# Attention weights of heads 16 to 29 transposed by DMA instead of TensorE, in a sorted-block attention followed by a dense mixture of experts

## The chip, the cores and the metric

The kernel runs on one core of a Trainium2 chip. Such a core has TensorE (PE in the profile: matmuls, and weight loads as PEld), VectorE (DVE), ScalarE (ACT), GpSimd (POOL), SyncE (SP, which here only issues DMAs) and 16 DMA engines. The metric is the device time of one execution in microseconds (us); several runs are taken, and their median counts.

## The reference

Four batches of 8 heads (32 heads, written g below), 768 positions, 64 columns a head. The positions form 8 blocks of 96. A sorting matrix P (8x8 for each head) is made doubly stochastic by five rounds of exponential and of row and column normalisation; it mixes the blocks of k and v; then each block of q attends to the sorted block in its place. The result, 3072 rows of 512, goes through 8 experts with weights P from a second normalisation (8 rounds). Every expert works on every row.

```python
k_sorted = einsum('bhij,bhjcd->bhicd', P, k_blocks)        # v the same
attn = softmax(q_block @ k_sorted_block.T / 8)             # 96 x 96 for each block and head
x = (attn @ v_sorted_block) as [B*S, H*D]                  # 3072 x 512
logits = x @ w_gate; P = exp(logits - max)
8 times: P /= row sums; P /= column sums; P *= N/E
out = sum over e of P[:, e] * (relu(x @ w1[e]) @ w2[e])    # 512 -> 1024 -> 512
```

Inputs and output are float32; the kernel computes its matmuls in bfloat16.

## The kernel before

The order of the instructions on every engine is the order in which the Python code emits them, up to the end of the gate's normalisation. Engines wait for each other through semaphores that the framework places for every tile. Each engine takes its own instructions strictly in order, so an instruction that waits holds whatever is behind it.

**Start.** GpSimd issues the loads of the first five pairs of heads (`load_pair`, k, v and q, cast to bfloat16 on the way). VectorE and ScalarE normalise P for all 32 heads at once.

**Attention loop.** Step s runs from 0 to 33. In it stand, in this order:

1. `scores(s)`: 8 matmuls into a psB tile (L310); VectorE takes row maxima (L315) and subtracts them (L317).
2. `a_transpose(s-1)`: 8 transposes on TensorE of the 96x96 blocks of attention weights into a psF tile (L328), and a ScalarE copy to `aT_` (L330).
3. `sort_kv(s+2)`: 6 matmuls mix the blocks of k and v (L295), ScalarE casts the result into `kvT_` (L298), and SP issues a DMA transpose that puts v into `v1_` (L301), 64 rows of 1024.
4. `weights(s)`: ScalarE's exponential into `at_` (L321).
5. On even steps `q_transpose` (L253, copies L259) and GpSimd's `relayout` (L78); on odd steps `x_transpose` of a finished pair of heads (L353, copy L356).
6. `attend(s-1)`, called AV below: 8 matmuls (L335), with a column of ones in v that gives the row sums; `normalise(s-1)` on VectorE (L343, L344).

**Buffers.** PSUM has two pools: psB with 2 buffers of two banks (scores, sort, AV in turn) and psF with 4 of one bank (all transposes, all pieces). `kvT_` holds 4 heads, `v1_` 5, `at_` and `aT_` 2 each; these are cut by hand out of one tile each, by head modulo the number. Raw pairs have 5 buffers.

**Pieces.** Expert 0 is computed inside the loop. Whenever eight heads of a batch are done, its 768 rows can be used: `add` puts a gate piece (L209), 16 first-layer pieces (L187, relu on ScalarE L190) and 6 output tiles (L198, copied to SBUF at L200) on a list, and says over how many slots they are to be spread. `fill()` stands four times in each step and is a slot: it emits pieces as their hand-given costs (0.65, 1.72, 0.7) fall due.

```python
def fill():
    if slots[0] > 0:
        ahead[0] += sum(c for c, _ in pieces) / slots[0]
        slots[0] -= 1
    while pieces and ahead[0] >= pieces[0][0] / 2:
        c, run = pieces.pop(0); run(); ahead[0] -= c
```

**Behind the loop.** The gate piece and the pieces of the fourth batch run beside the eight rounds of the gate's normalisation; then come experts 1 to 7, each with six stretches of 32 first-layer matmuls into hps (L417) and 32 second-layer ones into psF (L495). The weights have two buffers (`load_expert`, L163 and L164).

Of the kernel before, what the change touches and what calls it, by code (L numbers as in the profile page):

```python
# [12 lines left out]
BF16 = mybir.dt.bfloat16  # L13
# [6 lines left out]
def mkap(t, dims, off=0):  # L20
    return bass.AP(tensor=t.tensor, offset=t.offset + off, ap=dims)
# [3 lines left out]
def kernel(  # L25
# [11 lines left out]
    nc = tc.nc  # L37
    B, H, S, D = 4, 8, 768, 64
    NB, BL = 8, 96
    CL, CH = 6, 16  # L40
    NH = B * H
# [11 lines left out]
    pp = ctx.enter_context(tc.tile_pool(name="pp", bufs=1))  # L53
# [4 lines left out]

    rawp = ctx.enter_context(tc.tile_pool(name="rawp", bufs=5))
    iop = ctx.enter_context(tc.tile_pool(name="iop", bufs=2))
    raw_t, kv_t = {}, {}

    def load_pair(n):
        kv = rawp.tile([128, 2, 2, CL, D], BF16, name="kvr")
        qr = rawp.tile([128, 2, CL, D], BF16, name="qr")
        for t, r in ((k, kv[:, 0]), (v, kv[:, 1]), (q, qr)):
            nc.gpsimd.dma_start(
                out=r.rearrange("p h c d -> p h (c d)"),  # L70
                in_=bass.AP(tensor=t.tensor, offset=t.offset + 2 * n * S * D,
                            ap=[[CL * D, 128], [S * D, 2], [1, CL * D]]))
        raw_t[n] = (kv, qr)
# [23 lines left out]
    nc.vector.memset(P9, EPS)  # L97
    perp = ctx.enter_context(tc.tile_pool(name="perp", bufs=1))

    NKT, NVB = 4, 5  # L100
    kvT_ = perp.tile([128, NKT, NB, 128], BF16)
    nc.vector.memset(kvT_[:, :, :, 96:128], 0.0)

# [11 lines left out]
    nc.vector.memset(qT_[0:64, :, :, S:], 0.0)  # L115


    at_ = perp.tile([96, 2, S + 32], BF16)
    aT_ = perp.tile([97, 2, S + 32], BF16)
    nc.vector.memset(at_[:, :, S:], 0.0)  # L120
    nc.vector.memset(aT_[0:96, :, S:], 0.0)

    mask16 = ones.tile([128, CH], F32)
    nc.vector.reduce_sum(out=mask16, in_=If32.rearrange("p (j c) -> p c j", c=CH), axis=AX.X)
# [8 lines left out]
    for it in range(5):  # L133
# [9 lines left out]
        if it == 0:  # L143
            Ibf = ones.tile([128, 128], BF16)
# [15 lines left out]
    def load_expert(e):  # L160
        w1e = wp.tile([128, 4, F], BF16, name="w1e")
        w2e = wp.tile([128, 8, Dm], BF16, name="w2e")
        nc.gpsimd.dma_start(out=w1e, in_=moe_w1[e].rearrange("(kk k) f -> k kk f", k=128))  # L163
        nc.gpsimd.dma_start(out=w2e, in_=moe_w2[e].rearrange("(fb k) f -> k fb f", k=128))  # L164
        w1t.append(w1e)
        w2t.append(w2e)
# [14 lines left out]
    def l1_piece(c, fb):  # L181
        def run():
            if fb == 0:
                hT0[c] = mps.tile([128, 8, 512], BF16, name="hTs")
            hps = psF.tile([128, 512], F32, name="psF")
            for kk in range(4):
                nc.tensor.matmul(hps[:, 0:HC], w1t[0][:, kk, fb * 128:(fb + 1) * 128],  # L187
                                 xtT[:, kk, c * HC:(c + 1) * HC],
                                 start=(kk == 0), stop=(kk == 3))
            nc.scalar.activation(out=hT0[c][:, fb, 0:HC], in_=hps[:, 0:HC], func=AF.Relu)  # L190
        return run

    def l2_piece(c, tt, copy=nc.vector.tensor_copy):
        def run():
            t = c * 3 + tt
            oacc = psF.tile([128, Dm], F32, name="psF")
            for fb in range(8):
                nc.tensor.matmul(oacc, hT0[c][:, fb, tt * 128:(tt + 1) * 128],  # L198
                                 w2t[0][:, fb, :], start=(fb == 0), stop=(fb == 7))
            copy(osbl[:, t, :], oacc)  # L200
        return run

    def gate_piece(b):
        def run():
            gps = psF.tile([128, 512], F32, name="psF")
            for tl in range(6):
                t = b * 6 + tl
                for kk in range(4):
                    nc.tensor.matmul(gps[:, tl * E:(tl + 1) * E], xtT[:, kk, t * 128:(t + 1) * 128],  # L209
                                     wg[:, kk], start=(kk == 0), stop=(kk == 3))  # L210
            nc.vector.tensor_copy(glog[:, b * 6:(b + 1) * 6, 0:E],
                                  gps[:, 0:6 * E].rearrange("p (t e) -> p t e", e=E))
        return run

    def batch_pieces(b):

        out_ = []
        for c in (2 * b, 2 * b + 1):
            out_ += [(0.65, l1_piece(c, fb)) for fb in range(8)]
            out_ += [(1.72, l2_piece(c, tt)) for tt in range(3)]  # L220
        return out_

    pieces = []
# [2 lines left out]
    def add(more, n):  # L226

        pieces.extend(more)
        slots[0] = n
# [88 lines left out]
        ssb_t[g] = ssb  # L318

    def weights(g):  # L320
        nc.scalar.activation(out=at_[:, g % 2, 0:S].rearrange("p (i c) -> p i c", c=BL),  # L321
                             in_=ssb_t.pop(g).rearrange("p a i c -> p (a i) c"),
                             func=AF.Exp, scale=scale)

    def a_transpose(g):
        ta = psF.tile([128, NB, 96], BF16, name="psF")
        for i in range(NB):
            nc.tensor.matmul(ta[:, i, :], at_[:, g % 2, i * BL:i * BL + 128], Ibf[0:96, 0:96],  # L328
                             is_transpose=True, start=True, stop=True)
        nc.scalar.copy(aT_[0:96, g % 2, 0:S], ta[0:96].rearrange("p i c -> p (i c)"))  # L330

    def attend(g):
        ops_ = psB.tile([128, 2, 4, 128], F32, name="psB")
        for i in range(NB):
            nc.tensor.matmul(ops_[:, i // 4, i % 4, 0:65], aT_[0:97, g % 2, i * BL:i * BL + 128],  # L335
                             v1_[0:97, g % NVB, i, 0:65], start=True, stop=True)
        ops_t[g] = ops_

    def normalise(g):
        n, r0 = g // 2, 64 * (g % 2)  # L340
        ops_ = ops_t.pop(g)
        den = sp.tile([96, 2, 4], F32, name="den")
        nc.vector.reciprocal(out=den, in_=ops_[0:96, :, :, 64])  # L343
        nc.vector.tensor_mul(  # L344
            og_[:, n % 2, :, r0:r0 + 64].rearrange("p (a i) d -> p a i d", a=2),
            ops_[0:96, :, :, 0:64],
            mkap(den, [den.ap[0], [4, 2], [1, 4], [0, 64]]))

    def x_transpose(n):
        b, hp = n // 4, n % 4  # L350
        tx = psF.tile([128, NB, 96], BF16, name="psF")
        for i in range(NB):
            nc.tensor.matmul(tx[:, i, :], og_[:, n % 2, i, :], Ibf[0:96, 0:96],  # L353
                             is_transpose=True, start=True, stop=True)

        nc.scalar.copy(xtT[:, hp, b * S:(b + 1) * S].rearrange("p (i h l) -> p i h l", h=CH, l=CL),  # L356
                       tx.rearrange("p i (l h) -> p i h l", h=CH))

    build_R(nc.vector, Pps, 0, 2)
    nc.vector.tensor_copy(Pb, Pps[:, 0:256].rearrange("p (i g) -> p i g", g=32))  # L360
    nc.vector.memset(aT_[96:97], 1.0)
    sort_kv(0)
    build_R(nc.gpsimd, Pb, 2, 2)
    relayout(1)
    load_pair(5)
    nc.gpsimd.dma_start(out=wg, in_=moe_w_gate.rearrange("(kk k) e -> k kk e", k=128))
    NP = NH // 2
    for s in range(NH + 2):
        if s % 2 == 0 and s + 4 < NH:
            build_R(nc.gpsimd, Pb, s + 4, 2)  # L370
        if s < NH:
            scores(s)
        if s == 0:
            sort_kv(1)
            onesc = ones.tile([128, 128], F32)
            nc.gpsimd.memset(onesc, 1.0)
            nc.gpsimd.memset(glog[:, NT, :], EPS / 128)
            nc.gpsimd.memset(glog[:, 0:NT, E:E + 1], EPS)
        fill()
        if 0 <= s - 1 < NH:  # L380
            a_transpose(s - 1)
        fill()
        if s + 2 < NH:
            sort_kv(s + 2)
        if s < NH:
            weights(s)
        if s % 2 == 0:
            if 0 < s and s // 2 + 1 < NP:
                q_transpose(s // 2 + 1)
            if s // 2 + 2 < NP:  # L390
                relayout(s // 2 + 2)
        elif s >= 3:
            x_transpose((s - 3) // 2)
        fill()
        if 0 <= s - 1 < NH:
            attend(s - 1)
            normalise(s - 1)
        if s % 2 == 1 and s // 2 + 6 < NP:
            load_pair(s // 2 + 6)
        fill()  # L400
        if s % 8 == 1 and 1 < s < NH:
            add([(0.7, gate_piece((s - 9) // 8))] + batch_pieces((s - 9) // 8), 33)
        if s in (2, 20):
            load_expert(s // 16)
    actx.close()


# [54 lines left out]
    for it in range(8):  # L462
# [8 lines left out]
            out=gl, in0=gl, scalar=float(N) / E,  # L471
# [5 lines left out]
    for e in range(1, E):  # L477
        if e + 1 < E:
            load_expert(e + 1)
        for nc4 in range(6):  # L480
            for fb in range(AHEAD if (e, nc4) == (1, 0) else 0, 8):
                l1_tile(e, nc4, fb)
            for tt in range(4):
# [8 lines left out]
                for c0 in range(0, Dm, W):  # L492
                    oacc = psF.tile([128, Dm], F32, name="psF")
                    for fb in range(8):
# [3 lines left out]
                        out=osbl[:, t, c0:c0 + W], in0=oacc[:, 0:W],  # L498
                        scalar=glog[:, t, e:e + 1], in1=osbl[:, t, c0:c0 + W],
                        op0=ALU.mult, op1=ALU.add)  # L500
                    if e == E - 1:
                        nc.sync.dma_start(out=out[t * 128:(t + 1) * 128, c0:c0 + W],
                                          in_=osbl[:, t, c0:c0 + W])
# [30 lines left out]
```

## Time and profile before

| | |
|---|---|
| median of 3 runs | 765.98 us (765.73 to 766.4) |
| the profiled execution | 764.95 us |
| its span, first to last instruction | 763.2 us |
| mean granted TensorE clock | 0.993 |
| PE busy | 734.6 us (96%) |
| VectorE, ScalarE, GpSimd busy | 272.3, 338.6, 80.5 us (36, 44, 11%) |
| first scores; last AV of the loop | 15.9; 152.25 us |
| gate piece behind the loop | 156.29 us |
| first tile of expert 1; its second layer | 173.54; 186.3 us |

Times in a profile row are from the span's start. A timeline row reads: start, duration, engine, line, operation, what is written and read, shape, number of instructions; in brackets the idle time of the engine before it and what ended that. A row of the stretches reads: length, then for each engine the busy time and the number of instructions, the granted TensorE clock, the mean busy share of the DMA engines (counted in packets' time, so it can pass 1) and GB/s.

### The profile page before, as it was taken

The page shows a single profiled execution, that of the slowest core. Times are in us where ns is not written, and L with a number is a line of the kernel's source. Part 1 is how long each engine was busy: PE and PEld are TensorE (multiplying, and loading weights), DVE is VectorE, ACT ScalarE, POOL GpSimd, SP SyncE. Part 2 cuts the span into 40 slices and gives each one's busy share as a digit, 9 for nine tenths or more (in the row PEclk, how much of TensorE's full clock was granted, in tenths as well). Part 3 has the DMA queues.
Part 4 walks back from the last instruction along what each step waited for, and adds up shares of the span by engine and source line. Part 5 has one row for each costly group of instructions (what it writes and reads, how often), then busy time and mean ns, then how long its engine had stood idle before and what let it go on. Part 6 is the DMA issues. An engine that isn't in the chain of part 4 may idle for free.

```text
span 763.2 us, 10596 instructions
## 1 busy us (share of the span) xinstructions
PE 734.6 (96%) x4452; PEld 372.9 (49%) x4452; DVE 272.3 (36%) x466; ACT 338.6 (44%) x569; POOL 80.5 (11%) x104
## 2 busy tenths in 40 slices
PE   2779999999999999999999999999999999999998
PEld 2666666655444444444444444444444444444444
DVE  6878778666512112122121221221212212112122
ACT  7888888744342332423424334233243342432422
POOL 8954431000000000000000000000000000000000
PEclk9979999999999999999999999999999999999999
DMA  9999792205100420015000600042001500002112
GB/s 153 189 178 134 103 140 31 20 1 90 22 1 0 75 37 0 1 27 84 1 2 0 111 1 1 0 69 42 0 1 23 89 1 1 0 1 97 70 71 95
DMA packets 47231, 37.40 MB, mean 49 GB/s; under 512 B 19408, under 2 KB 40144, under 8 KB 47184
## 3 DMA queue, kind: packets, MB, share of 16 engines
q0 software_dynamic: 26128, 26.23, 22.5%
q1 hardware_dynamic: 21056, 10.50, 7.0%
q8 instruction: 35, 0.57, 0.3%
q14 instruction: 12, 0.10, 0.0%
HBM read 52.45 MB, written 6.29 MB: 77 GB/s over the span
## 4 chain that ended last, share of the span: by engine, by line
PE 93%; ACT 2%; DVE 2%; DMA 1%; issue 0%; DVEq 0%; ACTq 0%
PE psF L495 38%; PE hps L417 38%; PE psF L187 5%; PE psF L198 5%; DMA v__108<-kvT__106 1%; PE psF L328 1%; PE psB L310 1%; PE psB L295 1%; PE psB L335 1%; ACT kvT__106 L298 1%; ACT aT__115 L330 0%; DVE ssb L317 0%; PE psF L353 0%; PE psF L253 0%; DVE mx L315 0%
## 5 line engine op out<-in xcount | busy, mean ns | idle before, releaser
L420 ACT ACTIVATE hTs<-hps 128x512 bf16<-128x512 f32 x336 | 200.7, 597 | 372.8 <-PE hps L417 372.8
L417 PE MATMUL hps<-xtT,w1e 128*128 128x512 bf16 x1344 | 297.4, 379 | 0.0
L495 PE MATMUL psF<-w2e,hTs 128*128 128x512 bf16 (+1 forms) x1352 | 296.9, 378 | 0.0
L497 DVE SCALAR_TENSOR_TENSOR osbl<-psF,glog,osbl 128x512 f32<-128x512 f32 (+1 forms) x169 | 126.3, 748 | 437.6 <-PE psF L495 437.4
L495 PEld LDWEIGHTS <-hTs 128*128 128x128 bf16 x1352 | 132.4, 98 | 157.7
L417 PEld LDWEIGHTS <-w1e 128*128 128x128 bf16 x1344 | 131.5, 98 | 158.5
L187 PE MATMUL psF<-xtT,w1e 128*128 128x384 bf16 x256 | 50.7, 329 | 0.0
L163 POOL DMA_DIRECT2D w1e<-in_moe_w_dram x8 | 6.2, 774 | 420.9 <-PE hps L417 370.4
L198 PE MATMUL psF<-w2e,hTs 128*128 128x512 bf16 x192 | 45.4, 379 | 0.0
L190 ACT ACTIVATE hTs<-psF 128x384 bf16<-128x384 f32 x64 | 29.3, 508 | 5.5 <-PE psF L187 4.9
L317 DVE TENSOR_TENSOR ssb<-psB,mx 96x768 f32<-96x768 f32 x32 | 30.5, 954 | 3.2
L330 ACT COPY aT__115<-psF 96x768 bf16<-96x768 bf16 x32 | 25.9, 809 | 12.6 <-PE psF L328 12.5
L315 DVE TENSOR_REDUCE mx<-psB 96x8 f32<-96x768 f32 x32 | 30.3, 947 | 2.0 <-PE psB L310 1.5
L298 ACT CAST kvT__106<-psB 128x768 bf16<-128x768 f32 x32 | 26.1, 816 | 7.8 <-PE psB L295 7.3
L321 ACT ACTIVATE at__114<-ssb 96x768 bf16<-96x768 f32 x32 | 27.6, 864 | 2.0 <-DVE ssb L317 1.7
L187 PEld LDWEIGHTS <-w1e 128*128 128x128 bf16 x256 | 22.7, 98 | 11.3 <-issue 0.3
L198 PEld LDWEIGHTS <-hTs 128*128 128x128 bf16 x192 | 17.8, 100 | 17.1
L78 POOL COPY kv<-kvr 128x1536 bf16<-128x1536 bf16 x15 | 22.0, 1469 | 33.1 <-PE psB L295 19.8
L344 DVE TENSOR_TENSOR og__235<-psB,den 96x512 bf16<-96x512 f32 x32 | 22.0, 687 | 1.1
L335 PE MATMUL psB<-v__108,aT__115 97*128 97x65 bf16 x256 | 13.8, 199 | 7.9 <-ACT kvT__106 L298 3.2
L295 PE MATMUL psB<-R,kv 128*128 128x128 bf16 x192 | 18.7, 242 | 2.3 <-ACT kvT__106 L298 0.9
L253 PE MATMUL psF<-Ibf,qr 128*128 128x128 bf16 x96 | 9.5, 246 | 10.9 <-DMA qr<-in_q_dram 10.9
(81 smaller groups left out, 293.7 us busy)
## 6 DMA issues: line engine op xcount, KB each, us to landing
w1e<-in_moe_w_dram POOLq DMA_DIRECT2D x8, 1024.0 KB, 8.0
w2e<-in_moe_w_dram POOLq DMA_DIRECT2D x8, 1024.0 KB, 8.8
out_dram<-osbl SPq DMA_DIRECT2D x23, 256.0 KB, 2.0
kvr<-in_k_dram POOLq DMA_DIRECT2D x16, 192.0 KB, 6.4
kvr<-in_v_dram POOLq DMA_DIRECT2D x16, 192.0 KB, 6.7
qr<-in_q_dram POOLq DMA_DIRECT2D x16, 192.0 KB, 7.0
v__108<-kvT__106 SPq DMA_TRANSPOSE x32, 5.2
out_dram<-osbl SPq DMA_DIRECT2D x2, 128.0 KB, 1.8
```

The costliest lines, as they stand in the source:

```text
L187: nc.tensor.matmul(hps[:, 0:HC], w1t[0][:, kk, fb * 128:(fb + 1) * 128], xtT[:, kk, c * HC:(c + 1) * HC], start=(kk == 0), stop=(kk == 3))
L190: nc.scalar.activation(out=hT0[c][:, fb, 0:HC], in_=hps[:, 0:HC], func=AF.Relu)
L198: nc.tensor.matmul(oacc, hT0[c][:, fb, tt * 128:(tt + 1) * 128], w2t[0][:, fb, :], start=(fb == 0), stop=(fb == 7))
L295: nc.tensor.matmul(kvf[:, cl * 128:(cl + 1) * 128], kv[:, e * CL + cl].rearrange("p t d -> p (t d)"), R[:, g].rearrange("p i c -> p (i c)" ...
L298: nc.scalar.copy(kvT_[:, g % NKT, :, 0:96].rearrange("p i (l c) -> p i l c", c=CH), mkap(kvps, [kvps.ap[0], [CH, NB], [128, CL], [1, CH]]))
L315: nc.vector.reduce_max(out=mx, in_=s4, axis=AX.X)
L317: nc.vector.tensor_sub(ssb, s4, mkap(mx, [mx.ap[0], [4, 2], [1, 4], [0, 96]]))
L321: nc.scalar.activation(out=at_[:, g % 2, 0:S].rearrange("p (i c) -> p i c", c=BL), in_=ssb_t.pop(g).rearrange("p a i c -> p (a i) c"), fun ...
L417: nc.tensor.matmul(hps, w1t[e][:, kk, fb * 128:(fb + 1) * 128], xtT[:, kk, nc4 * 512:(nc4 + 1) * 512], start=(kk == 0), stop=(kk == 3))
L420: nc.scalar.activation(out=hT[e, nc4][:, fb, :], in_=hps, func=AF.Relu)
L495: nc.tensor.matmul(oacc[:, 0:W], hT[e, nc4][:, fb, tt * 128:(tt + 1) * 128], w2t[e][:, fb, c0:c0 + W], start=(fb == 0), stop=(fb == 7))
L497: nc.vector.scalar_tensor_tensor(out=osbl[:, t, c0:c0 + W], in0=oacc[:, 0:W], scalar=glog[:, t, e:e + 1], in1=osbl[:, t, c0:c0 + W], op0=A ...
```

## The change

- The weights of heads 16 to 29 (`DT`) no longer go through `a_transpose`. Behind their exponential, SP issues a DMA transpose from `at_` to `aT_`, 96 rows of 1024. `at_` now has 128 columns for each block, of which column 96 is 1 and the rest 0, so that row 96 of `aT_` comes out as the ones that AV needs.
- AV and normalise of these heads stand in step g+2 instead of g+1; the x transposes, and the pieces of a batch, follow the heads that they need.
- `at_` and `aT_` have 3 buffers instead of 2, `kvT_` 3 instead of 4, raw pairs 6 instead of 5. Pairs 11 to 15 are loaded in steps 10, 11, 13, 15, 17 instead of 11, 13, 15, 17, 19.
- The pieces of the three batches are added in steps 9, 17 and 26 (before: 9, 17, 25) and spread over 34, 40 and 28 slots (before: 33 each).
- The middle one of three output tiles is copied by ScalarE instead of VectorE in the second and third batch: four tiles in all.
- Expert 1 is loaded in step 31 instead of 20, behind a small GpSimd copy that reads the weights of head 31.

```diff
-    rawp = ctx.enter_context(tc.tile_pool(name="rawp", bufs=5))
+    rawp = ctx.enter_context(tc.tile_pool(name="rawp", bufs=6))
...
-    NKT, NVB = 4, 5
+    NKT, NVB = 3, 5
...
-    at_ = perp.tile([96, 2, S + 32], BF16)
-    aT_ = perp.tile([97, 2, S + 32], BF16)
-    nc.vector.memset(at_[:, :, S:], 0.0)
-    nc.vector.memset(aT_[0:96, :, S:], 0.0)
+    DT = range(16, NH - 2)
+    NAT, NTT = 3, 3
+    at_ = perp.tile([96, NAT, NB, 128], BF16)
+    aT_ = perp.tile([128, NTT, S + 32], BF16)
+    nc.vector.memset(at_[:, :, :, 96:128], 0.0)
+    nc.vector.memset(at_[:, :, :, 96:97], 1.0)
+    nc.vector.memset(aT_[:, :, S:], 0.0)
...
-            out_ += [(1.72, l2_piece(c, tt)) for tt in range(3)]
+            out_ += [(1.72, l2_piece(c, tt, nc.scalar.copy if c >= 2 and tt in (1,)
+                                     else nc.vector.tensor_copy)) for tt in range(3)]
...
     def weights(g):
-        nc.scalar.activation(out=at_[:, g % 2, 0:S].rearrange("p (i c) -> p i c", c=BL),
+        nc.scalar.activation(out=at_[:, g % NAT, :, 0:96],
                              in_=ssb_t.pop(g).rearrange("p a i c -> p (a i) c"),
                              func=AF.Exp, scale=scale)
+        if g in DT:
+            nc.sync.dma_start_transpose(
+                out=aT_[:, g % NTT, 0:S].rearrange("p (i c) -> p i c", c=BL),
+                in_=at_[:, g % NAT].rearrange("p i c -> p (i c)"))
...
-        nc.scalar.copy(aT_[0:96, g % 2, 0:S], ta[0:96].rearrange("p i c -> p (i c)"))
+        nc.scalar.copy(aT_[0:97, g % NTT, 0:S], ta[0:97].rearrange("p i c -> p (i c)"))
...
-    nc.vector.memset(aT_[96:97], 1.0)
...
+    step = {g: g + (2 if g in DT else 1) for g in range(NH)}
+    at_step = {}
+    for g in range(NH):
+        at_step.setdefault(step[g], []).append(g)
+    x_step = {}
+    for n in range(NP):
+        x_step.setdefault(max(step[2 * n], step[2 * n + 1]) + 1, []).append(n)
+    loads = {2 * n - 11: n for n in range(6, 11)}
+    loads.update({10: 11, 11: 12, 13: 13, 15: 14, 17: 15})
+    new = []
...
-        if 0 <= s - 1 < NH:
+        if 0 <= s - 1 < NH and s - 1 not in DT:
             a_transpose(s - 1)
...
-        elif s >= 3:
-            x_transpose((s - 3) // 2)
+        for n in x_step.get(s, []):
+            x_transpose(n)
+            if n % 4 == 3 and n < NP - 1:
+                new = [(0.7, gate_piece(n // 4))] + batch_pieces(n // 4)
         fill()
-        if 0 <= s - 1 < NH:
-            attend(s - 1)
-            normalise(s - 1)
-        if s % 2 == 1 and s // 2 + 6 < NP:
-            load_pair(s // 2 + 6)
+        for g in at_step.get(s, []):
+            attend(g)
+            normalise(g)
+        if s in loads:
+            load_pair(loads[s])
         fill()
-        if s % 8 == 1 and 1 < s < NH:
-            add([(0.7, gate_piece((s - 9) // 8))] + batch_pieces((s - 9) // 8), 33)
-        if s in (2, 20):
-            load_expert(s // 16)
+        if new:
+            add(new, {9:34,17:40,26:28}[s])
+            new = []
+        if s == 2:
+            load_expert(0)
+        if s == 31:
+            late_ = pp.tile([1, 8], BF16)
+            nc.gpsimd.tensor_copy(late_, at_[0:1, 31 % NAT, 0, 0:8])
+            load_expert(1)
```

More of the change, by code (lines that the diff above doesn't have):

```diff
@@ L327, in a_transpose @@
         for i in range(NB):
-            nc.tensor.matmul(ta[:, i, :], at_[:, g % 2, i * BL:i * BL + 128], Ibf[0:96, 0:96],
+            nc.tensor.matmul(ta[:, i, :], at_[:, g % NAT, i], Ibf[0:96, 0:96],
                              is_transpose=True, start=True, stop=True)
-        nc.scalar.copy(aT_[0:96, g % 2, 0:S], ta[0:96].rearrange("p i c -> p (i c)"))
+        nc.scalar.copy(aT_[0:97, g % NTT, 0:S], ta[0:97].rearrange("p i c -> p (i c)"))
     def attend(g):
@@ L334, in attend @@
         for i in range(NB):
-            nc.tensor.matmul(ops_[:, i // 4, i % 4, 0:65], aT_[0:97, g % 2, i * BL:i * BL + 128],
+            nc.tensor.matmul(ops_[:, i // 4, i % 4, 0:65], aT_[0:97, g % NTT, i * BL:i * BL + 128],
                              v1_[0:97, g % NVB, i, 0:65], start=True, stop=True)
```

## The prediction

> **What bounds the kernel now.** I read the page first: PE is busy 734.6 of 763.2 us, and from about 53 us on it hardly stops. The chain that ended last says the same: 93% PE, and after 186 us nothing but alternating first and second layers of experts 1 to 7, which the diff does not touch. So the question is when PE gets through the attention steps with the pieces of expert 0 in them. I took the stretches by the start of each step's scores (L310): steps 3 to 6 (26.62 to 39.94 us, no pieces yet), 10 to 16, 17 to 25, and 26 up to the gate piece behind the loop (156.29).
>
> ```profile
> core 0: us, PE busy (x) PEld busy (x) DVE busy (x) ACT busy (x) POOL busy (x), PEclk, DMA share, GB/s
> 26.62:39.94 13.32, 8.79 (x153) 7.69 (x150) 11.84 (x21) 12.08 (x19) 10.19 (x13) 1.00 1.20 194
> 51.09:83.12 32.03, 31.45 (x382) 22.61 (x380) 23.79 (x41) 27.32 (x48) 16.57 (x20) 0.93 1.02 137
> 83.12:124.46 41.34, 40.50 (x493) 27.77 (x490) 33.15 (x55) 34.19 (x59) 13.63 (x14) 1.00 0.72 103
> 124.46:156.29 31.83, 31.56 (x366) 21.20 (x364) 22.48 (x37) 23.54 (x41) 0.00 (x0) 1.00 0.19 20
> ```
>
> In the last two stretches PE has 98% and more, VectorE and ScalarE 70 to 83%. Without pieces (first row) it is the other way: a step takes 3.33 us, and VectorE and ScalarE are busy 89% and 91% of it.
>
> What a group costs PE is read from start to start, since busy times overlap:
>
> ```profile
> 101.56 0.50 PE L310 MATMUL psB<-kvT__106,qT__111 128*128 128x96 bf16 x8
> 101.90 0.51 PE L328 MATMUL psF<-Ibf,at__114 96*128 96x96 bf16 x8
> 102.25 1.89 PE L198 MATMUL psF<-w2e,hTs 128*128 128x512 bf16 x8
> ...
> 103.97 0.50 PE L295 MATMUL psB<-R,kv 128*128 128x128 bf16 x6
> 104.31 0.51 PE L353 MATMUL psF<-Ibf,og__235 96*128 96x96 bf16 x8
> ```
>
> Scores 0.34, weight transposes 0.345, an output tile 1.73, sort 0.34. In the same way AV is 0.245, q and x transposes 0.34 each, a first-layer piece 0.65, a gate piece 0.6. Setting these against the order that the code gives (the slots of fill() can be counted by hand), PE's work is 39.3 us in steps 17 to 25, which took 41.34 (2.0 lost), and 31.0 from step 26 on, which took 31.83 (0.85 lost).
>
> Last, the DMA transposes of v, the only ones there are, by source line, in the DMA view of 118 to 146 us, and in the chain:
>
> ```profile
> L301 SPq DMA_TRANSPOSE v__108<-kvT__106 x32: 1194/1196/2162, 15.9 to 141.0; - x32
> DMA to landing us min/median/max: 2.6/5.2/10.9
> ```
>
> ```profile
> q1 hardware_dynamic: 3264, 0.79, 25.9%
> ...
> v__108<-kvT__106 SPq DMA_TRANSPOSE x6, 2.7
> ```
>
> ```profile
> 32.75 10.89 DMA v__108<-kvT__106
> 43.64 0.14 issue
> 43.77 0.42 PE psB L335 x8
> ```
>
> Alone, a 64x1024 transpose lands in 2.7 us and holds the queue 1.2 us (25.9% of 28 us is 7.25 us of 16 engines, 1.2 for each of six). While expert 0 and the pairs load (DMA share 1.20 in the first row), it takes up to 10.9 and PE waits.
>
> **Part 1, PE transposes.** 14 heads x 0.345 = 4.83 us of PE go, all in stretches where PE is the bound. The 14 ScalarE copies (0.815 each, 11.4 us) lie beside PE; so do AV and x transposes, which only move. The pieces are the same. So the gain is 4.83 us less what is newly waited for.
>
> **Part 2, the new spread.** Counting the slots again: steps 9 to 16 hold the same PE work. Steps 17 to 25 lose nine transposes (3.1), three output tiles (5.2), one AV and one x transpose (0.6): 39.3 becomes 30.4. From step 26 on the three tiles and the AV and x come back and five transposes go: 31.0 becomes 35.0. In steps 17 to 25 the others have then as much to do. VectorE: nine max and subtract at 1.95 (start to start), eight reciprocal and multiply at 0.9, four q copies at 0.71, four tiles at 0.685, 0.2: 30.5 us. ScalarE: nine casts and exps at 1.68, four q copies at 0.95, four x copies at 0.8, 16 relus at 0.51, a tile at 0.59: 30.9. Three engines with 30.4 to 30.9 each, tied by two psB buffers (AV waits for the subtract, the next sort for the multiply), don't run without waits. Lower bound of the loss: 1.0, half of today's. Upper: if no engine carried anything over a step's end, the largest share of each step summed, 35.3, so 4.9. Nearest row: steps 3 to 6, VectorE and ScalarE 90% busy in the same ties, 30.7/0.9 = 34.1. The pieces are spread there, and ScalarE's psF work may lag, so I take 3.1, that is 1.1 more than today. From step 26 on PE has far more than the others (35.0 against some 24); I take 0.3 more than today, bounds 0 and 1. The four tiles on ScalarE (0.59 instead of 0.685 on VectorE) are in these sums.
>
> **Part 3, the DMA transposes.** SP gets, after v of head s+2, the weights of head s: 96x1024, 1.5 times as much. Bounds for the issue: 1.2 (as any) and 2.4 (twice); I take 1.8 by size. Landing: 2.7 and 10.9; by size 4.0 alone. SP has 3.0 of some 3.8 us a step then; v is behind it, but has two steps to spare. Exp ends about 4.3 us after its step's scores, AV stands 2.6 after the scores two steps on: 2x3.8+2.6-4.3 = 5.9 us. 4.0 plus up to 1.0 for the v transpose ahead fits. Cost 0. If that cover goes, AV holds PE and what is queued behind it, the next scores. The pairs that still load during steps 16 and 17 (v landed in 4.1 there, x1.5 = 6.2) may cost 0.3 once; that lies in the 1.1.
>
> The Trainium skill ("VectorE: DVE Perf Modes", The three transpose paths) speaks against this change: it has 1309 ns for a 128x128 on the DMA path against 390 on TensorE, and tells to use TensorE where PSUM will do. By it six such blocks are an estimated 7.9 us, 2.0 over the cover, and at the price in rival (c) the sum would be 6.5 us slower. The trace has four blocks' worth in 2.7 us, not 5.2, so I follow the trace.
>
> **Part 4, three kvT buffers.** The cast of head s+2 now overwrites head s-1, whose v transpose must have read it. The one of head 6 landed at 43.64, and the cast of head 9 started at 42.04: ScalarE would stand 1.6 us, and behind it are exp 7, an x copy and the weight copy. AV 6 waits for the same landing anyway, so part of it is covered. Bounds 0 and 1.3 (exp 7 from 43.14 to 44.46); I take 0.5. Three weight buffers, six raw buffers: POOL's waits for q (9.6 us) are behind relayouts that are early; 0.
>
> **Part 5, expert 1.** Its load goes from step 20 to behind exp 31 (now 148.3). On POOL only expert 2's load is queued behind it, which waits until 174.02 today. It lands 9.8 (w1) and 16.2 us (w2) after issue today; from about 147 that is 158 and 164, needed at some 170 and 183. Cost 0; without that cover, a us for each us late. At the start VectorE gets some 0.3 us of memsets before 2.4 us, covered by 0.7 us in which the first exp waits for ScalarE; the 1.39 us memset at L361 stood in front of a wait for PE: 0.
>
> **Sum.** 4.83 - 1.1 - 0.3 - 0.5 = 2.9 us. The profiled execution took 764.95 (span 763.2 and 1.75 around it), so 762.05; the median of the runs is 765.98, 1.03 above it, so 763.1.
>
> **Rivals.** (a) The three engines run past each other as today, and the kvT wait is covered: the whole 4.8, 761.2. For: PE lost only 2.0 us of 41 with ScalarE at 83%. Against: 30.4 against 30.5 and 30.9. (b) It is given back: loss 4.9 instead of 2.0, 1.3 at kvT, 0.3: 0.3 us left, 765.7. For: the 90% row. (c) Slower: the weights land later than AV. The loop AV, scores, exp, transpose, AV spans three steps, so each us beyond 5.9 costs a third of a us in each of 14 steps, 4.7 us; from a landing of 6.5 us it decides, and at 7.0 it is 5.2 - 2.9 = 2.3 us slower, 768.3. For: v landed in 8 to 10 us beside loads. Against: those loads are over by step 18, and 4.0 is far from 6.5.
>
> PE's clock adds to the range: 46 to 55 us ran at a granted 0.50, after a wait at 42 to 44 that the kvT change touches. Such a stretch 3.4 us longer or shorter where PE is the bound is 1.7 us either way.
>
> **Numbers.** Forecast 0.62; (a) 0.13; (b) 0.13; (c) 0.12. A measurement of this kernel can tell about 0.2%, 1.5 us, from no change: 764.45 and 767.5. The forecast's own spread puts a little into no change, (b) is no change with a small tail to either side, (c) slower: faster 0.72, same 0.15, slower 0.13. Range: at best 4.8 with 1.0 less loss, at worst (b) and a little beyond: 760.4 to 766.2.
>
> **What would show it.** L328 and L330 with 18 instead of 32 groups; steps 17 to 25 in 33 to 34 us, with VectorE and ScalarE over 88% busy and PE around 92%; from step 26 some 36 us; the gate piece at about 153.4; the new transposes landing in 4 to 5 us, and no wait of L335 for them. ScalarE waiting before a cast at about 42 us. I am wrong if L335 waits for DMA in many steps (c), if the first expert-1 tile waits for its weights, or if steps 17 to 25 take over 36 us (b).

## The result, and the profile after

The changed kernel takes 761.77 us (median of 6 runs, 760.26 to 762.65) against 765.48 us (764.67 to 766.4): ratio 0.9949, 95% interval 0.9934 to 0.9963, or 3.7 us faster, of which the interval leaves 2.8 to 5.1. 2.9 us had been forecast. The profiled execution took 760.26 us, its span is 758.5 us against 763.2.

Eighteen heads are left on TensorE, read from the groups of instructions up to 160 us (busy time, mean ns of one | idle before):

```profile
L341 ACT COPY aT__115<-psF 97x768 bf16<-97x768 bf16 x18 | 14.5, 806 | 5.6 <-PE psF L339 5.5
...
L339 PE MATMUL psF<-Ibf,at__114 96*128 96x96 bf16 x144 | 10.7, 226 | 1.6 <-ACT at__114 L328 1.4
```

The same four stretches as before, cut again at the starts of the scores of steps 3, 7 and 10, 17, 26 and at the gate piece behind the loop (columns as in the prediction's first fence):

```profile
26.63:40.62 13.99, 9.53 (x153) 8.09 (x151) 12.00 (x21) 12.19 (x19) 10.19 (x13) 0.89 1.20 195
51.41:82.82 31.41, 29.96 (x380) 21.46 (x380) 23.88 (x41) 27.72 (x49) 17.88 (x23) 1.00 1.18 156
82.82:116.37 33.55, 31.31 (x377) 21.61 (x377) 29.89 (x50) 26.68 (x48) 9.67 (x9) 1.00 0.61 95
116.37:152.03 35.66, 35.06 (x360) 22.35 (x364) 22.97 (x39) 24.14 (x42) 1.90 (x4) 1.00 0.45 82
```

Steps 17 to 25 went from 41.34 to 33.55 us, the rest of the loop from 31.83 to 35.66. PE is busy 93% of the third stretch, VectorE 89%, ScalarE 80%. From step 17 to the gate piece it is 73.17 before and 69.21 after: 4.0 of the 4.7 us between the two profiles. Of the others, 0.3 lie ahead of step 17 and 0.4 at the very end: in both profiles VectorE's last instruction starts 603.36 us behind the gate piece, and only what follows it up to the last instruction, with the last output's store in it, differs.

The new transposes, by their source line:

```profile
L332 SPq DMA_TRANSPOSE aT__115<-at__114 x14: 1212/1267/2384, 84.1 to 135.2; - x14
...
DMA to landing us min/median/max: 2.6/2.7/4.6
```

They land in 2.7 us by the median, in 4.6 at most, and nobody waits for them.

### The profile page after: what moved, and what is told of

Its sections match the earlier page's. It is cut to its first block, busy times and chain, and to the rows that moved or that the text cites. A ratio compares the mean times of both kernels' runs of the same rounds, so it can differ in the third digit from the quotient of the medians.

```text
span 758.5 us, 10311 instructions
## 1 busy us (share of the span) xinstructions
PE 725.8 (96%) x4274; PEld 367.7 (48%) x4340; DVE 268.3 (35%) x462; ACT 331.5 (44%) x559; POOL 80.6 (11%) x105
## 4 chain that ended last, share of the span: by engine, by line
PE 91%; ACT 3%; DVE 3%; DMA 1%; issue 1%; ACTq 0%; DVEq 0%
PE hps L445 38%; PE psF L523 38%; PE psF L203 5%; PE psF L192 5%; DMA v__108<-kvT__106 1%; PE psB L317 1%; PE psB L302 1%; ACT kvT__106 L305 1%; PE psB L346 1%; PE psF L339 1%; DVE ssb L324 1%; ACT at__114 L328 1%; DVE mx L322 0%; ACT qT__111 L266 0%; PE psF L364 0%
## 5 line engine op out<-in xcount | busy, mean ns | idle before, releaser
L192 PE MATMUL psF<-xtT,w1e 128*128 128x384 bf16 x256 | 49.0, 326 | 0.6 <-ACT qT__111 L266 0.6
L322 DVE TENSOR_REDUCE mx<-psB 96x8 f32<-96x768 f32 x32 | 30.4, 949 | 5.8 <-PE psB L317 5.4
L317 PE MATMUL psB<-kvT__106,qT__111 128*128 128x96 bf16 x256 | 18.0, 219 | 2.2 <-ACT kvT__106 L305 1.5
```

The costliest lines, as they stand in the source:

```text
L322: nc.vector.reduce_max(out=mx, in_=s4, axis=AX.X)
```

## The experiments

Single runs of one kernel lie 1 to 5 us apart. The profiles show one source of this: a stretch of half granted clock between 37 and 61 us whose place and length differ from execution to execution (last section). Six of the kernels below have the same instructions up to step 15 (the changed one, 3, 5, 6, 7 and 10), and in their profiles step 17 starts at 82.8, 84.4, 84.6, 87.5, 84.2 and 83.0 us. The profiles therefore say more than the medians from step 17 on: there, two kernels that differ only ahead of it agree within 0.02 us (the changed kernel and the one with four kvT buffers). The table has the ratio to the kernel before, and from each profile the time from the scores of step 17 to those of step 26, on to the gate piece, and from step 17 to the end.

| kernel | ratio (95%) | 17 to 26 | 26 to gate | 17 to end |
|---|---|---|---|---|
| before | 1 | 41.34 | 31.83 | 680.04 |
| changed | 0.9949 (0.9934 to 0.9963) | 33.55 | 35.66 | 675.67 |
| 1: no DMA transposes, even spread | 1.0011 (0.9998 to 1.0024) | 41.50 | 31.98 | 680.35 |
| 2: DMA transposes, even spread | 1.0014 (1.0005 to 1.0024) | 38.84 | 32.33 | 681.10 |
| 6: no DMA transposes, new spread | 1.0022 (1.0008 to 1.0037) | 37.27 | 36.59 | 680.72 |
| 9: as 2, x ahead of q | 0.9990 (0.9980 to 1.0000) | 38.69 | 30.16 | 678.79 |
| 3: AV one step after | 0.9991 (0.9980 to 1.0003) | 37.41 | 35.07 | 678.98 |
| 5: expert 1 in step 20 | 1.0052 (1.0037 to 1.0066) | 40.79 | 35.67 | 682.92 |
| 7: each transpose twice | 1.0237 (1.0212 to 1.0263) | 46.62 | 42.78 | 696.02 |
| 4: four kvT buffers | 0.9941 (0.9919 to 0.9964) | 33.53 | 35.65 | 675.65 |
| 10: tiles on VectorE | 0.9946 (0.9930 to 0.9961) | 34.08 | 35.91 | 676.46 |
| 8: from head 13 | 0.9978 (0.9965 to 0.9991) | 38.58 | 33.95 | 680.30 |
| candidate 1: filled steps | 0.9938 (0.9925 to 0.9950) | 36.76 | 33.53 | 676.77 |
| candidate 2: from 13, x ahead | 0.9959 (0.9946 to 0.9971) | 38.32 | 33.80 | 679.89 |

Experiments 2 and 9 leave 3.4 us of pieces behind the gate piece, so only their last column compares. Experiment 8 and both candidates put more or fewer pieces ahead of step 17 than the changed kernel, so for them the ratio decides, not the columns.

**1, 2 and 6: transposes and spread, each without the other.** Theory A: the 14 groups taken off TensorE bring the gain. Rival B: other edits do, expert 1's load above all. Rival C: the spread does.

```diff
-    DT = range(16, NH - 2)             # 1 and 6
+    DT = range(0)
-            add(new, {9:34,17:40,26:28}[s])
+            add(new, 33)                       # 1 and 2
+            add(new, {9:34,17:40,25:32}[s])    # 6
```

> No head's weights go by DMA: all 32 by TensorE with AV one step later as in the kernel before, pieces over 33 slots each; all other edits stay (three kvT buffers, six raw buffers, earlier loads, expert 1 in step 31, one tile in three on ScalarE). Theory A, the gain is the 14 transposes taken off TensorE: 4.8 us of PE work return, so it is at the kernel before or up to 0.5 us slower (ratio 1.000 to 1.001). Rival B, the gain comes from the other edits, expert 1's load out of the middle above all: it stays 2 to 4 us faster than before (0.995 to 0.998).

> As the changed kernel, but the three batches' pieces are spread over 33 slots each, as before. By the slots, batch 1 then ends in step 25, step 26 has no pieces (1.6 us of PE work in a step in which VectorE has 3.5), and 3.4 us of pieces are left behind the loop. Theory A: the spread is worth 1 us, so 2.5 to 3 us faster than before (ratio 0.996 to 0.997). Rival C, the spread carries the gain, since without it PE is idle whenever VectorE and ScalarE limit: no faster than before by more than 1 us (0.999 to 1.000).

> The missing fourth corner: no head's weights go by DMA (AV one step later for all, as before), but the pieces are spread as in the changed kernel, over 34, 40 and 32 slots; all other edits stay. The even spread gave 1.0011 without and 1.0014 with the DMA transposes, the changed kernel 0.9949. Theory A2, both are needed: without the transposes' relief TensorE is the bound in every step and the spread only moves its work, so 1.000 to 1.002. Rival C, the spread alone brings the gain: 0.995 to 0.998.

Without the transposes the gain is gone (680.35 and 680.72 against 680.04), whatever the spread: B falls, and C as "the spread alone" falls too. But the transposes with the even spread bring nothing either: 681.10. That is 5.4 us over the changed kernel; A had expected 1, and rival C as experiment 2 puts it, that without the spread no more than 1 us is gained, came nearer. So the gain needs both. PE's work counted as in the prediction, experiment 2 loses 3.2 us in steps 17 to 25 (38.84 for 35.7 of work), as much as the changed kernel, but 6.0 from step 26 to the gate piece (32.33 for 26.3), where the changed kernel loses 0.7. Its timeline shows these 5.4 us, at the turn from batch 1 to batch 2:

```profile
123.60 0.51 PE L364 MATMUL psF<-Ibf,og__236 96*128 96x96 bf16 x8
...
125.44 0.84 ACT L328 ACTIVATE at__114<-ssb 96x768 bf16<-96x768 f32 x1 [1.13 <-DVE ssb L324]
...
126.19 0.94 ACT L266 COPY qT__111<-psF 64x384 bf16<-64x384 bf16 x2
...
127.16 0.80 ACT L367 COPY xtT<-psF 128x768 bf16<-128x768 bf16 x1
...
128.01 0.70 PE L214 MATMUL psF<-wg,xtT 128*128 128x8 bf16 x21 [2.00 <-ACT xtT L367]
```

PE made the x transpose at 123.6, ScalarE copied it at 127.16: ahead of it in ScalarE's order stood the exp, which waited for VectorE, and two q copies. With 33 slots the pieces of batch 1 are used up at that point, so PE has nothing but the gate piece, and that reads this copy. The clock follows, in the stretches of the same run:

```profile
122.59:125.46 2.87, 1.92 (x38) 1.71 (x36) 2.56 (x4) 0.82 (x2) 0.00 (x0) 1.00 0.31 70
125.46:131.91 6.45, 4.46 (x54) 3.21 (x54) 4.14 (x9) 4.38 (x7) 0.00 (x0) 0.74 0.28 67
```

By the order of the code, step 26 (2.86 us, the first row) holds 1.6 of PE work, so 1.3 are lost; then come 2.0 of waiting and 3.4 us at a granted 0.5 (128.2 to 131.7), of which half, an estimated 1.7, is lost. That is 5.0 of the 5.4. In the changed kernel 34 and 40 slots do not fit between two batches (32 and 36 are there), so pieces are left over and cover the copy: its profile has no wait of L214 from 55 us to the gate piece.

**9: the same with the copy earlier.** The x transpose is put ahead of the q transpose in a step, so ScalarE's copy of x no longer stands behind the q copies.

```diff
-        if s % 2 == 0:
-            ... q_transpose, relayout
         for n in x_step.get(s, []):
             ...
+        if s % 2 == 0:
+            ... q_transpose, relayout
```

> The even spread of 33 slots once more, but in each step the x transpose stands ahead of the q transpose, so that on even steps ScalarE's copy of x, for which a new batch's gate piece waits, no longer stands behind two q copies of 0.95 us together. Theory: in the even spread PE stood 2.0 us at the gate piece of batch 2 with nothing else to do, and TensorE ran at half clock for 3.4 us after it; with the copy 1 us earlier the wait halves, and 1 to 3 us of the 5 lost against the changed kernel come back (ratio to before 0.997 to 1.000). Rival: what is lost is the thin step 26 and VectorE's chain alone, and the order changes nothing (1.001 to 1.002).

```profile
PE psF L214 <- ACT xtT L367: 1.0, 1, 1.0
```

The wait halved, the clock no longer fell there, and 2.3 us came back (681.10 to 678.79), step 27 going from 6.46 to 4.42 us. The mechanism is shown; the thin step 26 (2.86 us again, 1.3 lost) and the 1.0 left of the wait remain. That is 2.3 of the 3.1 us by which it is still behind the changed kernel; 0.8 stays open.

**3 and 5: the cover of the landing.**

```diff
-    step = {g: g + (2 if g in DT else 1) for g in range(NH)}     # 3
+    step = {g: g + 1 for g in range(NH)}
-        if s == 2:                                               # 5
-            load_expert(0)
-        if s == 31:
-            late_ = ...
-            load_expert(1)
+        if s in (2, 20):
+            load_expert(s // 16)
```

> As the changed kernel, but AV of heads 16 to 29 stands one step after the weights (g+1), so only about 2.1 us (3.8 + 2.6 - 4.3) lie between the exp's end and AV, while the transpose lands in 2.6 to 2.7 us from its issue. Theory A: PE waits 0.5 to 1.5 us at most AVs, and as the wait closes a loop in every step it comes back in every one: 5 to 15 us slower than the changed kernel, so 2 to 11 us slower than before (ratio 1.002 to 1.015). Rival: a landing of 2.7 us is hidden anyway by the pieces ahead of AV, and it is within 1 us of the changed kernel (0.994 to 0.997).

> As the changed kernel, but expert 1 is loaded in step 20 as before, so its 4 MB come from HBM while transposed weights are wanted. In the kernel before the v transposes issued beside that load landed in 5.6 to 8.6 us instead of 2.7. Theory A: for three or four heads the weights land 2 to 3 us past the cover of 5.9 us less the queue; PE waits 3 to 6 us in all, so 0 to 2 us slower than before (ratio 1.000 to 1.003). Rival: AV has enough room, PE waits under 1 us and it stays 2.5 to 4 us faster than before (0.995 to 0.997).

In experiment 3 (batches spread over 34, 40 and 32 slots, the third added in step 25 instead of 26) the landing is the same 2.6 us and PE waits for it, from the waits of 60 to 160 us (total, times, longest):

```profile
PE psB L346 <- DMA aT__115<-at__114: 4.9, 6, 1.3
```

It costs 3.3 us (675.67 to 678.98), between the two expectations (5 to 15, or under 1): six waits, not fourteen. The step of delay is needed, but it is a matter of 3 us. In experiment 5 the landing itself grows, and PE waits for it once (the waits of 92 to 116 us, then two stretches):

```profile
L332 SPq DMA_TRANSPOSE aT__115<-at__114 x14: 1212/1241/5472, 85.2 to 144.2; - x14
...
DMA to landing us min/median/max: 2.8/3.4/12.0
```

```profile
PE psB L346 <- DMA aT__115<-at__114: 5.3, 1, 5.3
```

```profile
97.40:106.80 9.40, 5.17 (x52) 3.06 (x49) 4.85 (x8) 5.66 (x10) 2.40 (x3) 0.94 1.11 182
106.80:112.40 5.60, 4.27 (x24) 2.27 (x25) 2.71 (x4) 0.00 (x0) 0.00 (x0) 0.50 1.25 206
```

Beside expert 1's weights the transposes of three heads land in 12.0, 11.2 and 6.6 us. One AV waits 5.3 us (102.8 to 108.1); within that wait the granted clock falls to 0.50, and it stays there until 112.6. It costs 7.3 us (675.67 to 682.92), more than the whole gain and more than the 4 to 6 that were expected against the changed kernel. This is rival (c) of the prediction, made to happen: moving the load to step 31 is what keeps it away.

**7: twice the transposes.**

```diff
         if g in DT:
-            nc.sync.dma_start_transpose(...)
+            for _ in range(2):
+                nc.sync.dma_start_transpose(...)
```

> As the changed kernel, but SP issues each DMA transpose of weights twice to the same place; the second waits for the first to land, so the weights are there 5.2 to 5.4 us after the exp instead of 2.7, and SP is held that long. Theory: the cover is 5.9 us on average, so AV waits under 0.5 us at a few heads: 0 to 2 us slower than the changed kernel (ratio to before 0.995 to 0.998). Rival: the cover is thinner than worked out (steps of 3.5 us, exp late): PE waits about 1 us in most of 14 steps, 4 to 10 us slower than the changed kernel (1.000 to 1.008).

```profile
90.30 5.46 SPq L333 DMA_TRANSPOSE aT__115<-at__114  x2
...
95.86 1.22 SPq L308 DMA_TRANSPOSE v__108<-kvT__106  x1
```

```profile
PE psB L347 <- DMA aT__115<-at__114: 14.6, 11, 3.1
```

Both expectations missed: 20.4 us. It did not test the cover. The second transpose waits on SP for the first, the pair holds the queue 3.8 to 5.7 us, and the v transpose of the next head stands behind it. With 1.25 for that, SP has 5.1 to 7.0 us a step where the changed kernel's step takes 3.7. From 89 to 162 us its queue has no gap of over 0.1 us, and the steps last 5.7 on average, so SP sets them. Three of PE's waits, of 3.1, 2.7 and 3.0 us, have a stretch of 3.4 us at half granted clock behind them (from 97.6, 114.6 and 131.7 us), an estimated 1.7 us lost for each, which is part of the 20.4. What it shows is how near SP's order is to the path: the one transpose holds it 1.27 us and leaves room, a wait in it does not.

**4 and 10: small parts.** Four kvT buffers (and two of at, to make room); and all tiles on VectorE.

```diff
-    NKT, NVB = 3, 5            # 4
+    NKT, NVB = 4, 5
-    NAT, NTT = 3, 3
+    NAT, NTT = 2, 3
-   nc.scalar.copy if c >= 2 and tt in (1,) else nc.vector.tensor_copy    # 10
+   nc.scalar.copy if c >= 99 else nc.vector.tensor_copy
```

> As the changed kernel, but four kvT buffers as before (and two at buffers, to make room; a weight buffer is read 2.7 us after its exp and written two steps later). Theory of part 4: the casts of heads 7, 8 and 9 no longer wait for a v transpose (1.5 us in three waits), and scores of step 10 start 0.3 us earlier; a difference that the times can't show: 0.993 to 0.997. Rival: three kvT buffers cost more, by shifting the whole loop: 1 us or more faster than the changed kernel (0.990 to 0.993).

> As the changed kernel, but all output tiles inside the loop are copied by VectorE; the four on ScalarE go back. Theory: in steps 17 to 25 VectorE's chain sets thin steps, and one of the four tiles (0.685 us) lies there, the others in steps that TensorE sets: 0 to 0.7 us slower than the changed kernel (ratio to before 0.995 to 0.997). Rival: it is worth more, 1 us or more slower (0.997 to 0.999).

The changed kernel's waits from 26 to 56 us have the line below; with four buffers it is gone, and step 10 starts at 51.17 instead of 51.41 us. Putting the tiles back costs 0.8 us by the profile (675.67 to 676.46), a little over the 0.7 expected; the medians show neither.

```profile
ACT kvT__106 L305 <- DMA v__108<-kvT__106: 1.5, 3, 0.8
```

**8 and the candidates: more heads, fuller steps.**

```diff
-    DT = range(16, NH - 2)
+    DT = range(13, NH - 2)                          # 8 and candidate 2
-            add(new, {9:34,17:40,26:28}[s])
+            add(new, {9:36,18:34,26:27}[s])         # 8 and candidate 2
+            add(new, {9:36,17:39,26:28}[s])         # candidate 1
```

Both candidates also have experiment 4's buffers and experiment 9's order.

> As the changed kernel, but heads 13 to 29 go by DMA (17 instead of 14) and the pieces are added in steps 9, 18 and 26 over 36, 34 and 27 slots, which leaves fewer steps with less than 3.5 us of TensorE work. Theory: three more groups of 0.345 us, and 0.5 us less idle in thin steps: 1 to 1.5 us faster than the changed kernel (ratio to before 0.992 to 0.994). Rival: in steps 13 to 15 the pairs still load, the weights land late, or the gate piece of batch 1 waits for its x copy: 0 to 4 us slower than the changed kernel (0.995 to 1.000).

> A candidate: the changed kernel with four kvT buffers (two at buffers), x ahead of q in a step, and the pieces over 36, 39 and 28 slots, so that step 17 holds 4.5 instead of 2.7 us of TensorE work and step 25 4.6 instead of 2.9, and the last batch still finds left-over pieces ahead of its gate piece. Theory, steps under 3.5 us of TensorE work are where it idles: 0.5 to 1.5 us faster than the changed kernel (ratio to before 0.992 to 0.994). Rival: two output tiles in one step cost as much by their own waits: within 0.5 us of it (0.994 to 0.996).

> A candidate: heads 13 to 29 by DMA with 36, 34 and 27 slots, as in the run from head 13, now with x ahead of q in a step and four kvT buffers (two at buffers). That run was 2 us slower than the changed kernel, with PE standing 2.4 us at gate pieces. Theory: half of that wait goes and the kvT wait too: 1.5 to 3 us faster than that run (ratio to before 0.994 to 0.996), and faster than the changed kernel only if the whole wait goes (0.992). Rival: the late weights of heads 13 to 16 (4.0 to 6.3 us) are what it lost by: no change against that run (0.997 to 0.999).

Experiment 8 is 2 us slower than the changed kernel (ratios 0.9978 and 0.9949, intervals apart). Its late landings (6.3, 4.0, 4.6, 5.0 us for heads 13 to 16) hardly matter: PE waits 0.2 us for them. It stands at its gate pieces again, since 36 and 34 slots leave almost no pieces over (36 and 32 are there):

```profile
PE psF L214 <- ACT xtT L367: 2.4, 2, 1.5
```

Candidate 2 has 1.4 us of that wait left and 762.73 us, ratio 0.9959 (0.9946 to 0.9971): by the medians one us of the two came back, though the intervals of the two touch. That more heads by DMA pay is not shown. Candidate 1 has 761.13 us, ratio 0.9938 (0.9925 to 0.9950). That is the lowest median of all; its interval overlaps the changed kernel's, so it beats the kernel before, and that it beats the changed one is not shown.

## Why the prediction was right

- **Part 1.** The gain comes from the 14 groups off TensorE: without them it is gone (experiments 1 and 6). The price of 0.345 us a group fits: from step 17 to the gate piece 4.83 - 1.1 - 0.3 = 3.4 us were forecast, 4.0 came, and the losses of the two stretches were 0.5 smaller than taken.
- **Part 2.** 33 to 34 us were forecast for steps 17 to 25 and 36 behind; 33.55 and 35.66 came. The loss was 3.1 (33.55 - 30.4), as taken; behind it 0.65 instead of 1.15. That 3.1 was hit so closely is in part luck, for ScalarE was 80% busy, not over 88. Its sum of 30.9 added the durations of single instructions; in the profile after they add to 30.1 in this stretch, but they overlap, and cover 26.7. VectorE has 89%, as foreseen. A mean hides what bounds: which engine is nearly full changes from step to step. Steps 17, 21, 22 and 25 hold 2.7 to 3.3 us of PE work each and took 3.5 to 3.8:

```profile
82.82:86.28 3.46, 2.91 (x36) 1.82 (x33) 3.32 (x6) 1.54 (x4) 0.83 (x1) 1.00 0.89 149
97.41:101.14 3.73, 3.40 (x35) 2.14 (x35) 2.49 (x4) 3.69 (x8) 1.69 (x2) 1.00 0.38 88
101.14:104.88 3.74, 3.48 (x51) 2.42 (x47) 3.59 (x7) 1.86 (x4) 0.38 (x1) 1.00 0.69 65
112.60:116.38 3.78, 3.15 (x36) 2.15 (x35) 3.03 (x5) 3.74 (x9) 1.41 (x1) 1.00 0.74 90
```

VectorE is busy 96% of steps 17 and 22, ScalarE 99% of 21 and 25. These four lose 2.4 of the 3.1 us, and step 19, with ScalarE busy 3.75 of 3.98 us, another 0.45. The chain of work that ended last, followed back from step 26, runs through VectorE from 82.8 to 86.2 us and through ScalarE from 110.9 to 116.3. In step 17, with 2.74 us of PE work, the next scores wait for VectorE's subtract:

```profile
85.27 0.95 DVE L324 TENSOR_TENSOR ssb<-psB,mx 96x768 f32<-96x768 f32 x1
...
86.28 0.51 PE L317 MATMUL psB<-kvT__106,qT__111 128*128 128x96 bf16 x8 [0.55 <-DVE ssb L324]
```

- What part 2 lacked: that the gain needs the new spread. It was costed as work moved between steps. Experiment 2 shows that an even spread would have made this change a loss, by a wait for the x copy that the trace of before does not have, since there x and q copies stand in different steps.
- **Part 3.** The landing was sized by rows, 4.0 us and 1.8 on SP; it is 2.7 and 1.27, hardly more than for 64 rows. The cost of 0 was right with more room than thought. The Trainium skill ("VectorE: DVE Perf Modes", The three transpose paths) has 1309 ns for one 128x128 block; the estimate of 7.9 us for six does not agree with the 2.7 us measured here, and the row decided. Rival (c) was priced at 4.7 us for each us beyond 5.9 in all 14 steps; experiment 5 has it for three heads, at 7.3 us.
- **Part 4.** 0.5 us taken; ScalarE waits 1.5 us in three waits, and step 10 shows 0.25 to 0.3 of it.
- **Part 5.** Expert 1's load in step 31 costs nothing: its first tile did not wait. That the move is worth 7.3 us was not worked out, since only its cost was asked.
- **Clock.** The half-clock stretch came at 37 to 48 us in the profile after instead of 45 to 56; step 10, which had 6.36 us, has 5.30, and so the 0.3 lost at step 10 turned into 0.3 gained at step 17. It was named as 1.7 us either way, so which way it went is luck.
- **The rest.** 4.7 us between the profiles against 2.9 forecast: 0.6 of the difference lies from step 17 to the gate piece, 0.8 ahead of step 17 (0.3 gained instead of 0.5 lost), and 0.4 behind the last output tile. That 0.4 is there in the profiles of experiments 3, 4, 5 and 10 and not in 1 and 6, which have no DMA transposes; its cause stays open.

## What to carry to other kernels

Work taken off the bounding engine turns into time only where something else is ready to take its place: look for the next wait at every turn of a schedule, and leave filler over there, rather than spreading it to the last piece. When a small transfer becomes part of the dependency chain, what it shares the DMA engines with matters more than its own size: 2.7 us alone, 12 beside a weight load. And count what a moved load protects, not only what its move costs.

## What the runs showed of the hardware

- A DMA transpose of 96x1024, with nothing beside it, takes hardly longer than one of 64x1024: 2.6 to 2.7 us to landing against 2.5 (2.6 to 2.7 in the kernel before), and 1.21 to 1.28 us on SP's queue against 1.20.
- TensorE's granted clock falls to 0.5 in stretches of 3.4, 6.8, 10.2 or 13.7 us. Behind step 17 of these runs and ahead of the last output tile it did so in five places, each time in or right behind a wait of PE of 2.0 us (experiment 2), 5.3 (experiment 5) or 2.7 to 3.1 (experiment 7); the single waits of 1.0 to 1.5 us there (experiments 3, 7, 8 and 9) had none behind them. In the loading phase, between 37 and 61 us, it also came behind a shorter wait (1.7 us, ending at 43.8 us, in the kernel before), and its place changes between executions; where it ends late, at 61.4 in experiment 6, step 10 takes 8.2 us instead of 5.3. The two profiles, before and after:

```profile
45.50:55.80 10.30, 9.02 (x113) 7.89 (x110) 7.62 (x13) 7.22 (x12) 8.01 (x10) 0.50 1.32 180
```

```profile
37.40:47.70 10.30, 8.68 (x98) 7.77 (x95) 8.45 (x14) 8.35 (x13) 3.86 (x5) 0.50 1.30 178
```
